# An opening on a fixed plan: eight units of attention ahead of the steps, engines in program order up to chunk 2

## The chip, the core and the metric

The kernel runs on one core of a Trainium2 chip. The metric is device time in microseconds (us). The median of three runs of the kernel before is 949.6 us (948.06 to 950.32). One further execution was recorded by the profiler; all durations and waits below are from it.

## What is computed

Windowed attention over 8 sequences of 576 tokens with 8 heads of 64 channels, followed by a feed-forward layer on the 4608 tokens:

```python
rel = pos[:, None] - pos[None, :]
mask = (rel >= 0) & (rel < 64)
scores = np.where(mask, scale * np.matmul(q, k.transpose(0, 1, 3, 2)), -1e9)
scores = scores - np.max(scores, axis=-1, keepdims=True)
attn = np.exp(scores)
attn = attn / (np.sum(attn, axis=-1, keepdims=True) + 1e-09)
x = np.matmul(attn, v)                      # to (4608 tokens, 512 channels)
h = x @ w_in                                # (512, 2048), drawn as float64
g = h * np.tanh(softplus(h))                # Mish
out = (g @ w_out).astype(np.float32)        # (2048, 512), float64
```

## The kernel before

**Chunks, units, steps.** The tokens are cut into 12 chunks of 384. A chunk's attention is four *units*, one for each pair of heads (NPAIR = 4). Its feed-forward part is 16 *steps*, one for each 128 rows of the hidden layer (NF = 16).

**A unit** is: TensorE makes six 128x128 squares of scores in PSUM (tile `s_ps`); VectorE adds the mask, scales, and keeps the row minimum (L148); ScalarE takes the exponential and the row sums (L151); VectorE adds 1e-9 to the sums, inverts them and multiplies (L155 to L157); the probabilities `pr` are transposed into `pT`; TensorE multiplies by V into `o_ps`; ScalarE rounds the result to `xh` (L250), and VectorE forms the rest `xl` (L251). The transposition is six TensorE transposes into `t_ps` with one copy by ScalarE and one by VectorE (L239, L240) in chunks 0 to 2. From chunk 3 on it is one VectorE transpose of 32x32 blocks into `tr` and twelve DMAs that move the blocks to `pT` (L190, L232).

**A step** has a first half (`ffn_in`): 12 matmuls of 384 columns into `h_ps`, namely xh and xl against the high part of w_in, and xh against its low part. ScalarE then computes Mish twice (`t`, L266, and its rounded `gh`, L267), and GpSimd the difference `gl` (L268). The second half (`ffn_out`, called by `flush`) is 9 matmuls of 512 columns into the accumulators `acc`. It runs LAG = 2 steps behind the first half.

**Weights.** They arrive as float64 in 32 *pieces* of 128x512, 16 of w_in and 16 of w_out, in staging tiles `st`. A piece is turned into two float32 tiles by five bit operations (`wa`, L298 to L303; the one at L299 is on GpSimd for a w_in piece, on VectorE for a w_out piece), one rounding on ScalarE (`wi_h` or `wo_h`, L304) and one subtraction (`wi_l` on VectorE, `wo_l` on GpSimd, L305).

**PSUM** has eight banks: three for the accumulators `acc0` to `acc2`, two for `h_ps`, three called `at`. Chunk 1's accumulators lie in the three `at` banks, since the steps of chunks 0 and 1 alternate and share the weights as they come.

**What sets the order.** The opening calls chunk 0's four units one after another; then HEAD = 5 steps of chunk 0 run alone while chunk 1's units are planned between them, and then steps of chunks 0 and 1 alternate: (0, f), (1, f - 5). Two pieces of weights are started at each step of chunk 0. Chunk 2's units are planned over the last steps of chunk 1. Up to there the tile framework's scheduler decides where an instruction stands in its engine's queue, with priorities (`high_priority`) as hints; only TensorE's steps are tied to the order of the program, through `in_order` once `ordered` is set. Every load goes through SyncE's queue. Chunks 3 to 11 follow the event list (`plan`, `plan_runs`).

Of the kernel before, what the change touches and what calls it, by code (L numbers as in the profile page):

```python
# [27 lines left out]
def tile_window_attn_mish_ffn(  # L28
# [109 lines left out]
    def probs(c, s_ps, turns):  # L138

        pr = ap_.tile([P, HM, P], F32, name="pr", bufs=2)  # L140
        mx = ap_.tile([P, HM], F32, name="mx", bufs=3)
        sm = ap_.tile([P, HM], F32, name="sm", bufs=3)
        for turn in turns:
            js = [h * NM + m for h, m in turn]
            for j, (h, m) in zip(js, turn):
                first = [(c * NB + 2 * m + par) % blocks_per_seq == 0 for par in range(2)]
                mk = firsts[first.index(True)] if any(first) else mask
                nc.vector.tensor_tensor_reduce(  # L148
                    out=pr[:, j, :], in0=s_ps[h][m], in1=mk,
                    op0=ALU.add, op1=ALU.min, scale=-0.125, scalar=3.0e38, accum_out=mx[:, j:j + 1])  # L150
                nc.scalar.activation(pr[:, j, :], pr[:, j, :], AF.Exp, bias=mx[:, j:j + 1], scale=-1.0,  # L151
                                     accum_out=sm[:, j:j + 1])
            js = slice(min(js), max(js) + 1)
            w = js.stop - js.start
            nc.vector.tensor_scalar(sm[:, js], sm[:, js], 1e-9, None, ALU.add)  # L155
# [352 lines left out]
```

## Time and profile before

| what | value |
|---|---|
| median of three runs | 949.6 us |
| the profiled execution | 949.47 us |
| its span, first to last instruction | 947.2 us |
| TensorE busy | 913.1 us, 96% of the span |
| VectorE busy | 312.3 us, 33% |
| ScalarE busy | 404.6 us, 43% |
| GpSimd busy | 241.9 us, 26% |
| start of the first `h_ps` matmul | 38.14 us |
| start of chunk 2's first `h_ps` matmul | 209.78 us |
| start of chunk 3's first `s_ps` matmul | 222.46 us |

PE is TensorE, PEld its loads of the stationary operand, DVE VectorE, ACT ScalarE, POOL GpSimd and SP SyncE. In the rows, a time in front is a start in us from the span's start, and the next number a length in us. A group's row gives busy us and mean ns of one, then idle time just before them and what ended it. Starts of neighbouring matmuls lie closer than their lengths, since matmuls are pipelined; the time that a run of them takes is read from start to start. Each float32 matmul of the attention stands twice in the trace (24 for the 12 of a unit).

### The profile page before, as it was taken

To read this page: it belongs to the slowest core of one execution; us is meant where nothing else is said; L and a number is where in the kernel's file an instruction comes from. 1 tells how busy PE (TensorE), PEld (TensorE's weight loads), DVE (VectorE), ACT (ScalarE), POOL (GpSimd) and SP (SyncE) were. 2 spreads that over 40 slices of the span, in tenths; PEclk is the share of its full clock that TensorE was granted. 3 is DMA by queue.
4 is the path that set the end of the run, shared out by engine and by line. 5 is a ranking of instruction groups with operands and counts; after the bars stand their busy time and mean duration, and the time that the engine had idled before them with its cause. 6 is when DMAs were issued, how large, how long until landed. Compare 5 with 4: busy or idle time off the path is not lost.

```text
span 947.2 us, 16773 instructions
## 1 busy us (share of the span) xinstructions
PE 913.1 (96%) x6408; PEld 816.2 (86%) x6408; DVE 312.3 (33%) x1016; ACT 404.6 (43%) x1116; POOL 241.9 (26%) x241
## 2 busy tenths in 40 slices
PE   4679999999999999999999999999999999999998
PEld 3568999878889999999999999999999999999997
DVE  6899885242331321312303303303203213210000
ACT  4574333565662543534525525525425435332211
POOL 2233565202112222222222222222122222222221
PEclk9779999999999999999999999999999999999999
DMA  7554441141331221212213204203302312200000
GB/s 252 157 198 144 134 133 45 54 120 63 94 105 59 84 80 62 80 55 90 78 29 117 75 23 123 75 26 94 106 26 84 114 27 81 82 26 1 34 1 34
DMA packets 82639, 77.26 MB, mean 82 GB/s; under 512 B 10368, under 2 KB 73856, under 8 KB 82560
## 3 DMA queue, kind: packets, MB, share of 16 engines
q1 hardware_dynamic: 77376, 66.75, 23.1%
q10 hardware_dynamic: 5184, 9.44, 2.7%
q8 instruction: 51, 0.84, 0.4%
q14 instruction: 28, 0.23, 0.1%
HBM read 56.10 MB, written 9.44 MB: 69 GB/s over the span
## 4 chain that ended last, share of the span: by engine, by line
PE 92%; DVE 5%; ACT 1%; SPq 1%; DMA 1%; issue 0%; ACTq 0%; DVEq 0%
PE h_ps L96 42%; PE acc L96 42%; PE o_ps L96 4%; PE s_ps L96 4%; DVE pr L157 1%; DVE pr L148 1%; DVE wa L302 1%; DVE wa L303 1%; ACT pr L151 1%; SPq L190 0%; PE t_ps L239 0%; DVE wi_l L305 0%; DMA k_t<-kT 0%; DVE wa L301 0%; ACT L266 0%
## 5 line engine op out<-in xcount | busy, mean ns | idle before, releaser
L268 POOL TENSOR_TENSOR gl<-t,gh 128x384 fp32r<-128x384 f32 x192 | 199.7, 1040 | 615.0 <-ACT gh L267 605.1
L266 ACT ACTIVATE t<-h_ps 128x384 f32<-128x384 f32 x192 | 94.4, 492 | 421.0 <-PE h_ps L96 405.9
L96 PE MATMUL h_ps<-xh,wi_h 128*128 128x384 f32 x768 | 261.2, 340 | 0.0
L96 PE MATMUL h_ps<-xh,wi_l 128*128 128x384 f32 x768 | 260.0, 339 | 0.0
L96 PE MATMUL h_ps<-xl,wi_h 128*128 128x384 f32 x768 | 259.0, 337 | 0.0
L96 PE MATMUL acc<-wo_h,gh 128*128 128x512 f32 x576 | 229.1, 398 | 0.0
L96 PE MATMUL acc<-wo_l,gh 128*128 128x512 f32 x576 | 227.5, 395 | 0.0
L96 PE MATMUL acc<-wo_h,gl 128*128 128x512 f32 x576 | 224.6, 390 | 0.0
L96 PEld LDWEIGHTS h_ps<-xh,wi_h 128*128 128x128 f32 x768 | 145.0, 189 | 9.3 <-issue 0.7
L96 PEld LDWEIGHTS h_ps<-xl,wi_h 128*128 128x128 f32 x768 | 145.1, 189 | 7.0
L96 PEld LDWEIGHTS h_ps<-xh,wi_l 128*128 128x128 f32 x768 | 144.9, 189 | 0.0
L96 PEld LDWEIGHTS acc<-wo_h,gl 128*128 128x128 f32 x576 | 108.6, 188 | 24.4 <-issue 0.2
L96 PEld LDWEIGHTS acc<-wo_h,gh 128*128 128x128 f32 x576 | 108.3, 188 | 20.8 <-issue 3.6
L96 PEld LDWEIGHTS acc<-wo_l,gh 128*128 128x128 f32 x576 | 108.6, 189 | 14.9
L151 ACT ACTIVATE pr<-pr,mx 128x128 f32<-128x128 f32 x288 | 111.7, 389 | 14.4 <-DVE mx L148 14.1
L219 DVE CAST xh<-o_ps 128x256 fp32r<-128x256 f32 x16 | 6.8, 425 | 326.9 <-PE o_ps L96 326.9
L267 ACT ACTIVATE gh<-h_ps 128x384 fp32r<-128x384 f32 x192 | 93.2, 485 | 0.0
L148 DVE CUSTOM_DVE_ANT_0 pr<-s_ps,mask 128x128 f32<-128x128 f32 x288 | 63.6, 285 | 32.0 <-PE s_ps L96 32.0
L286 DVE COPY o<-acc 128x512 f32<-128x512 f32 x12 | 8.3, 691 | 185.5 <-PE acc L96 185.5
L96 PE MATMUL s_ps<-k_t,q_t 64*64 64x128 f32 x1152 | 47.0, 291 | 11.8 <-DMA k_t<-kT 9.7
L151 ACT ACTIVATION_READ_ACCUMULATOR pr<-pr,mx 128x1 f32 x288 | 53.9, 187 | 0.0
L96 PEld LDWEIGHTS o_ps<-pT,v_t 128*64 128x64 f32 x1152 | 39.9, 146 | 15.6 <-issue 8.1
(43 smaller groups left out, 547.9 us busy)
## 6 DMA issues: line engine op xcount, KB each, us to landing
v_t<-vN SPq DMA_DIRECT2D x48, 384.0 KB, 4.0
k_t<-kT SPq DMA_DIRECT2D x47, 224.0 KB, 4.4
pT<-tr SPq DMA_DIRECT2D x432, 24.0 KB, 1.8
out<-o ACTq DMA_DIRECT2D x36, 256.0 KB, 2.3
q_t<-qT SPq DMA_DIRECT2D x47, 192.0 KB, 4.3
st<-w_in SPq DMA_DIRECT2D x16, 512.0 KB, 4.3
st<-w_out SPq DMA_DIRECT2D x16, 512.0 KB, 3.3
q_t<-qT SPq DMA_DIRECT2D x3, 64.0 KB, 2.1
```

The lines of the kernel that those rows point to most:

```text
L96: order.append(nc.tensor.matmul(*args, **kw).ins)
L148: nc.vector.tensor_tensor_reduce(out=pr[:, j, :], in0=s_ps[h][m], in1=mk, op0=ALU.add, op1=ALU.min, scale=-0.125, scalar=3.0e38, accum_out ...
L151: nc.scalar.activation(pr[:, j, :], pr[:, j, :], AF.Exp, bias=mx[:, j:j + 1], scale=-1.0, accum_out=sm[:, j:j + 1])
L157: nc.vector.tensor_tensor(pr[:, js, :], pr[:, js, :], sm[:, js].unsqueeze(2).to_broadcast([P, w, P]), ALU.mult)
L219: nc.vector.tensor_copy(xh[:, :cut], o_ps[0])
L266: nc.scalar.activation(t, h_ps, AF.Mish)
L267: nc.scalar.activation(gh, h_ps, AF.Mish)
L268: nc.gpsimd.tensor_tensor(gl, t, gh.bitcast(F32), ALU.subtract)
L286: nc.vector.tensor_copy(o, acc[t])
L302: nc.vector.scalar_tensor_tensor(a, hi, 0xC0000000, a, ALU.bitwise_and, ALU.bitwise_or)
L303: nc.vector.scalar_tensor_tensor(a, lo, 29, a, ALU.logical_shift_right, ALU.bitwise_or)
```

## The change

The first part of the program is written out in the order in which it is to run, and each instruction on VectorE, ScalarE, GpSimd and SyncE that goes through the wrapper `InTurn` keeps its place on its engine (`keep_in_program_order`) as long as `held[0]` is set, that is through step 31. TensorE is tied to the program's order from its first matmul.

The eight units of chunks 0 and 1 come first, in one loop over u. In turn u, VectorE masks unit u, finishes `xl` of unit u - 2, converts weight piece u and normalizes unit u; ScalarE rounds `xh` of unit u - 2, takes four exponentials of unit u, makes both copies of unit u - 1's transposes, and then the other two exponentials; TensorE makes the scores of unit u + 1, the values of unit u - 1 and the transposes of unit u. The first halves of steps 0 and 1 stand in turns 6 and 7. Steps of chunks 0 and 1 alternate from step 2 on (HEAD = 2). Each step converts one piece, and all VectorE work on it: the bit operations and the subtraction that GpSimd did have moved there, save one bit operation (`Abs`), which ScalarE does in the opening. Eight pieces are converted in the opening and 24 in steps 0 to 23.

Chunk 2's scores stand after steps 8, 11, 17 and 20, in the two `h_ps` banks, with an extra `flush` behind them; its exponentials come in two batches of twelve, at steps 11 and 20. Its transposes are VectorE's, at steps 14, 17, 22 and 24, so that 24 TensorE transposes fall away and 48 small DMAs are added. Its values come at steps 29 to 32.

```diff
     order = []
     ordered = []
+    held = [True]
+
...
+        def __getattr__(self, name):
+            call = getattr(self.engine, name)
+
+            def issue(*args, **kw):
+                i = call(*args, **kw)
+                if held[0]:
+                    tc.keep_in_program_order(i)
+                return i
+            return issue
+
+    vec, act, pool, load = (InTurn(e) for e in (nc.vector, nc.scalar, nc.gpsimd, nc.sync))
...
     def in_order():
-        return tc.issue_after(order[-1]) if ordered else nullcontext()
-
-
-
-
-    sums = itertools.cycle([f"acc{t}" for t in range(NTT)])
-
-    def bank(c, p, name):
-        if c == 2 or (c == 0 and p % 2 == 0):
-            return ps_acc.tile([P, CH], F32, name=name, tag=next(sums))
+        return tc.issue_after(order[-1]) if order else nullcontext()
+
+
+
+
+    def acc_bank(t, name):
+        return ps_acc.tile([P, CH], F32, name=name, tag=f"acc{t}")
+
+    def h_bank(name):
+        return ps_h.tile([P, CH], F32, name=name, tag="h_ps")
+
+    def at_bank(name):
         return ps_at.tile([P, CH], F32, name=name, tag="at")
...
+    def masked(c, unit, s_ps, squares_, exps=True):
+        pr, mx, sm = unit
+        for h, m in squares_:
+            j = h * NM + m
+            first = [(c * NB + 2 * m + par) % blocks_per_seq == 0 for par in range(2)]
+            mk = firsts[first.index(True)] if any(first) else mask
+            vec.tensor_tensor_reduce(
+                out=pr[:, j, :], in0=s_ps[h][m], in1=mk,
+                op0=ALU.add, op1=ALU.min, scale=-0.125, scalar=3.0e38, accum_out=mx[:, j:j + 1])
+            if exps:
+                exp(unit, [(h, m)])
...
-    def run_transpose(pr):
-        pT = next(pTs)
-        tr = mp.tile([P, P // 32, HM, 32], F32, name="tr", tag="st", bufs=3)
-        nc.vector.transpose(tr.rearrange("p k j i -> p j k i"), pr.rearrange("p j (k i) -> p j k i", i=32))
+    def run_transpose(pr, pT=None):
+        tr = mp.tile([P, P // 32, HM, 32], F32, name="tr", tag="st", bufs=3) if pT is None else             ap_.tile([P, P // 32, HM, 32], F32, name="tr", tag="v_t", bufs=2)
+        pT = pT or next(pTs)
+        vec.transpose(tr.rearrange("p k j i -> p j k i"), pr.rearrange("p j (k i) -> p j k i", i=32))
         return pT, moves(pT, tr)
+
+    def spare_pT():
+        pT = mp.tile([P, P // 32, HM, 32], F32, name="pT", tag="st", bufs=3)
+        pool.memset(pT, 0.0)
+        return pT
...
+    def te_transpose(pr, banks):
+        pT = next(pTs)
+        banks = [squares(b) for b in banks]
+        for h, t_ps in enumerate(banks):
             for m in range(NM):
                 order.append(nc.tensor.transpose(t_ps[:, m, :], pr[:, h * NM + m, :], ident).ins)
-            (nc.scalar.copy if h == 0 else nc.vector.tensor_copy)(
-                pT[:, :, h * NM:(h + 1) * NM, :].rearrange("p r m i -> p m r i"),
-                t_ps.rearrange("p m (r i) -> p m r i", i=32))
+        return pT, banks
+
+    def te_copies(pT, banks, by):
+        for h, (t_ps, copy) in enumerate(zip(banks, by)):
+            copy(pT[:, :, h * NM:(h + 1) * NM, :].rearrange("p r m i -> p m r i"),
+                 t_ps.rearrange("p m (r i) -> p m r i", i=32))
...
-        nc.vector.tensor_scalar(a, hi, 0x7FFFFFFF, None, ALU.bitwise_and)
-        (nc.gpsimd if first else nc.vector).tensor_scalar(af, af, BIG, TINY, ALU.min, ALU.max)
-
-        nc.vector.tensor_scalar(a, a, 3, 0x3FFFFFFF, ALU.logical_shift_left, ALU.bitwise_and)
-        nc.vector.scalar_tensor_tensor(a, hi, 0xC0000000, a, ALU.bitwise_and, ALU.bitwise_or)
-        nc.vector.scalar_tensor_tensor(a, lo, 29, a, ALU.logical_shift_right, ALU.bitwise_or)
-        nc.scalar.copy(wh, af)
-        (nc.vector if first else nc.gpsimd).tensor_tensor(wl, af, wh.bitcast(F32), ALU.subtract)
...
+        if by_act:
+            act.activation(af, hi.bitcast(F32), AF.Abs)
+        else:
+            vec.tensor_scalar(a, hi, 0x7FFFFFFF, None, ALU.bitwise_and)
+        worked.append((lo, hi, a, af, wh, wl))
+
+    def w_bits(parts=range(4)):
+
+        if not worked:
+            return
+        lo, hi, a, af, wh, wl = worked[0]
+        for part in parts:
+            if part == 0:
+                vec.tensor_scalar(af, af, BIG, TINY, ALU.min, ALU.max)
+            elif part == 1:
+                vec.tensor_scalar(a, a, 3, 0x3FFFFFFF, ALU.logical_shift_left, ALU.bitwise_and)
+            elif part == 2:
+                vec.scalar_tensor_tensor(a, hi, 0xC0000000, a, ALU.bitwise_and, ALU.bitwise_or)
+            else:
+                vec.scalar_tensor_tensor(a, lo, 29, a, ALU.logical_shift_right, ALU.bitwise_or)
+                rounded.append([af, wh, wl, False])
+                worked.pop(0)
+
+    def w_round():
+        for r in rounded:
+            if not r[3]:
+                act.copy(r[1], r[0])
+                r[3] = True
+
+    def w_rest():
+        while rounded and rounded[0][3]:
+            af, wh, wl, _ = rounded.pop(0)
+            vec.tensor_tensor(wl, af, wh.bitcast(F32), ALU.subtract)
...
-    HEAD = 5
+    HEAD = 2
...
+    def products_of(u):
+        a, p = units[u]
+        if u == 0:
+            banks = [b for t in range(NM) for b in ([acc_bank(0, "s_ps"), acc_bank(1, "s_ps")], [at_bank("s_ps"), at_bank("s_ps")],
+                                                     [h_bank("s_ps"), h_bank("s_ps")])[t]]
+        elif u % 2 == 0:
+            banks = [acc_bank(t, "s_ps") for t in range(2)]
+        else:
+            banks = [at_bank("s_ps") for _ in range(2)]
+        a.products(p, banks)
+        if u + 2 < U + 2:
+            a.load(p + 2, "qk")
+
+    def values_of(u):
+        a, p = units[u]
+        o_ps = (at_bank if u == U - 1 else lambda n: acc_bank(2, n))("o_ps")
+        outs[u] = o_ps
+        with in_order():
+            value_products(a.v[p], a.pT.pop(p), [o_ps[:, n:n + BLK] for n in range(0, CH, BLK)])
+        if u + 2 < U:
+            a.load(p + 2, "v")
...
-    take_w(1)
+    w_load()
     atts[0].load(1, "qk")
     atts[0].load(0, "v")
-    take_w(1)
+    w_load()
     atts[0].load(1, "v")
-    ev = []
-    for p in range(NPAIR):
-        ev += [(p, 2, atts[0].scores, p), (p + 0.75, 1, atts[0].transpose, p), (p + 1.25, 0, atts[0].values, p)]
-    for at, _, fn, p in sorted(ev, key=lambda e: e[:2]):
-        fn(p)
-        if at == p and p > 0:
-            take_w(1)
-    atts[1].plan(0, 2 * HEAD / (NPAIR + 1), 1, 1.5)
-    atts[2].plan(third, (starts[2] - third) / (NPAIR + 1), 1, 1.5)
-
+    w_load()
+
...
+    products_of(0)
+    for u in range(U + 1):
+        now = u < U
+        if u > 1:
+            rest_high(u - 2)
+        if now:
+            a, p = units[u]
+            squares_ = BY_PAIR if u == 0 else BY_HEAD
+            a.masked(p, squares_, exps=False)
+            exp(a.pr[p], squares_[:4])
+        if u == 0:
+            w_abs(False)
+        if u > 1:
+            rest_low(u - 2)
+        if u + 1 < U:
+            products_of(u + 1)
+        if u > 0:
+            units[u - 1][0].te_copies(units[u - 1][1], (act.copy, act.copy))
+            values_of(u - 1)
+        if u >= EARLY and len(early) < HEAD:
+            early.append(first_half(len(early)))
+        if now:
+            exp(a.pr[p], squares_[4:])
+        if u == U - 1:
+            for n, h_ps in enumerate(early):
+                step(n, h_ps)
+        w_bits([0])
+        w_rest()
+        w_bits([1, 2])
+        n = normal_parts(u) if now else iter(())
+        next(n, None)
+        w_bits([3])
+        next(n, None)
+        if u == U:
+            rest_high(u - 1)
+            rest_low(u - 1)
+        if u + 1 not in WITHOUT:
+            w_abs(u + 1 < U)
+            w_load()
+        next(n, None)
+        w_round()
+        if now:
+            a.te_transpose(p, [at_bank("t_ps") if u == U - 1 else acc_bank(h, "t_ps") if u == U - 2 else h_bank("t_ps") for h in range(2)])
 
...
+    third = atts[2]
+    SCORES = [8, 11, 17, 20]
+    MOVED = [14, 17, 22, 24]
+
+    def between(n):
+
+        if n in SCORES:
+            p = SCORES.index(n)
+            third.products(p, [h_bank("s_ps") for _ in range(2)])
+            third.load(p + 2, "qk")
+            with in_order():
+                flush()
+            third.masked(p, BY_HEAD, exps=False)
+            if p % 2:
+                third.exp(p - 1)
+                third.exp(p)
+                third.normal(p - 1)
+                third.normal(p)
+        if n in MOVED:
+            p = MOVED.index(n)
+            third.dve_transpose(p, p > 1)
+
     for n, (c, f) in enumerate(steps):
...
+        if n == starts[2] // 2:
+            held[0] = True
+            third.values(NPAIR - 1, h_bank)
+            with in_order():
+                flush()
+            held[0] = False
+        if n >= HEAD:
+            step(n)
         run(2 * n)
+        if held[0]:
+            w_round()
+            w_bits()
+            w_abs(False)
+            w_load()
+            if last - 3 <= n < last - 1:
+                third.load(n - last + 3, "v")
+            if last < n < last + NPAIR:
+                third.values(n - last - 1, h_bank)
         if len(pend) > LAG:
             with in_order():
                 flush()
+        if held[0]:
+            between(n)
+            w_rest()
         run(2 * n + 1)
-        if c == 0:
-            take_w(2)
```

What this makes of the queues is shown at three places. In these rows a tile's number tells buffers apart, and all instructions that pass through the wrapper carry its line, L106. `ISA pr,mx` is the masking of one square.

TensorE, the opening. Before:

```order
L96 MATMUL s_ps<-k_t,q_t 64x128 x24
L239 MATMUL t_ps<-ident,pr 128x128 x6
L96 MATMUL s_ps<-k_t,q_t 64x128 x12
L96 MATMUL o_ps<-pT_106,v_t 64x64 x12
L239 MATMUL t_ps<-ident,pr 128x128 x6
L96 MATMUL o_ps<-pT_107,v_t 64x64
L96 MATMUL s_ps<-k_t,q_t 64x128 x12
L96 MATMUL o_ps<-pT_107,v_t 64x64 x11
L239 MATMUL t_ps<-ident,pr 128x128 x6
```

TensorE, the same place, changed:

```order
L115 MATMUL s_ps<-k_t,q_t 64x128 x24
L288 MATMUL t_ps<-ident,pr 128x128 x6
L115 MATMUL s_ps<-k_t,q_t 64x128 x12
L115 MATMUL o_ps<-pT_106,v_t 64x64 x12
L288 MATMUL t_ps<-ident,pr 128x128 x6
L115 MATMUL s_ps<-k_t,q_t 64x128 x12
L115 MATMUL o_ps<-pT_107,v_t 64x64 x12
L288 MATMUL t_ps<-ident,pr 128x128 x6
```

The scores of unit u + 1 now always stand between the transposes and the values of unit u - 1, and the round repeats for eight units instead of four.

VectorE, a stretch of the opening that ends with the normalization of a unit. Before, in chunk 0's third unit:

```order
L298 TENSOR_SCALAR wa<-st 128x512
L305 TENSOR_TENSOR wi_l<-wa,wi_h 128x512
L301 TENSOR_SCALAR wa<-wa 128x512
L157 TENSOR_TENSOR pr<-pr,sm 128x384
L155 TENSOR_SCALAR sm<-sm 128x3
L251 TENSOR_TENSOR xl_245<-o_ps,xh_244 128x384
L302 SCALAR_TENSOR_TENSOR wa<-st,wa 128x512
L298 TENSOR_SCALAR wa<-st 128x512
```

VectorE, the third unit in the changed kernel, from behind its six masked squares:

```order
L106 TENSOR_TENSOR xl_293<-o_ps,xh_292 128x384
L106 TENSOR_SCALAR wa<-wa 128x512
L106 TENSOR_TENSOR wi_l<-wa,wi_h 128x512
L106 TENSOR_SCALAR wa<-wa 128x512
L106 SCALAR_TENSOR_TENSOR wa<-st,wa 128x512
L106 TENSOR_SCALAR sm<-sm 128x6
L106 SCALAR_TENSOR_TENSOR wa<-st,wa 128x512
L106 RECIPROCAL sm<-sm 128x6
L106 TENSOR_TENSOR pr<-pr,sm 128x768
```

The normalization is one pass over six squares instead of two over three, and the operations on one piece stand between `xl` and the normalization, one piece to a unit.

VectorE, steps 7 and 8 of the changed kernel (nothing in the kernel before answers to this place, since chunk 2's scores stood behind the last piece):

```order
L106 TENSOR_TENSOR wo_l<-wa,wo_h 128x512
L106 TENSOR_SCALAR wa<-wa 128x512 x2
L106 SCALAR_TENSOR_TENSOR wa<-st,wa 128x512 x2
L106 TENSOR_SCALAR wa<-st 128x512
L106 ISA pr,mx<-s_ps,mask 128x128
```

Six masked squares then stand between the bit operations of one piece and the subtraction of the piece before it. On TensorE, everything from chunk 3's first scores on stands in the same order in both kernels, row for row.

More of the change, by code (lines that the diff above doesn't have):

```diff
@@ L136, in products @@
                q_t[rows, n * BLK:(n + 1) * BLK], k_t[rows, n * BLK:n * BLK + P], start=True, stop=True)
[L138 to L155, printed above, removed]
-            nc.vector.reciprocal(sm[:, js], sm[:, js])
-            nc.vector.tensor_tensor(pr[:, js, :], pr[:, js, :], sm[:, js].unsqueeze(2).to_broadcast([P, w, P]), ALU.mult)
-        return pr
@@ L162, in squares, with probs, score_products @@
+    def probs(c, s_ps, squares_):
+        unit = new_probs()
+        masked(c, unit, s_ps, squares_)
+        normal(unit, squares_)
+        return unit[0]
+    BY_HEAD = [(h, m) for h in range(2) for m in range(NM)]
+    BY_PAIR = [(h, m) for m in range(NM) for h in range(2)]
     def squares(bank_):
         return bank_.rearrange("p (m k) -> p m k", k=P)
-    def att_scores(c, p, tiles):
-        s_ps = [squares(bank(c, p, "s_ps")) for _ in range(2)]
-        s_ps = [[s[:, m, :] for m in range(NM)] for s in s_ps]
+    def score_products(tiles, banks):
+        if len(banks) == 2:
+            s_ps = [squares(b) for b in banks]
+            s_ps = [[s[:, m, :] for m in range(NM)] for s in s_ps]
+        else:
+            s_ps = [[squares(banks[2 * m + h])[:, 0, :] for m in range(NM)] for h in range(2)]
@@ L168, in att_scores @@
         for m in range(NM):
             products(tiles, m, [s[m] for s in s_ps])
-        return probs(c, s_ps, HEADS if c == 0 else [sum(HEADS, [])])
+        return s_ps
+    def att_scores(c, p, tiles):
+        return probs(c, score_products(tiles, [at_bank("s_ps") for _ in range(2)]), BY_HEAD)
     def run_scores(c, qk):
@@ L419, in tile_window_attn_mish_ffn @@
         steps += [(0, f), (1, f - HEAD)]
-    third = 2 * len(steps) + 2
+    last = len(steps) - 2
     steps += [(1, f) for f in range(NF - HEAD, NF)]
@@ L428, in tile_window_attn_mish_ffn, with first_half, step @@
+    def first_half(n):
+        c, f = steps[n]
+        with in_order():
+            return ffn_in(c, atts[c].x, f)
+    def step(n, h_ps=None):
+        pend.append((*steps[n], function(h_ps or first_half(n))))
     atts[0].load(0, "qk")
[L429 removed]
+    w_load()
     atts[0].load(1, "qk")
     atts[0].load(0, "v")
[L432 removed]
+    w_load()
     atts[0].load(1, "v")
[L434 to L436 removed]
```

168 lines of the change are left out of this document (112 added, 56 removed).

## The prediction

> **What bounds the kernel now.** I read the page first, then the busy times by stretch, then TensorE's waits up to chunk 3.
>
> ```profile
> PE   4679999999999999999999999999999999999998
> PEclk9779999999999999999999999999999999999999
> ```
>
> The 40 slices show one engine at its limit from about 75 us on, TensorE. Only the first three slices leave it idle, and there its granted clock is low as well. Stretches cut at the changes of the clock:
>
> ```profile
> 0.00:27.20 27.20, 13.94 (x159) 10.09 (x159) 19.67 (x76) 11.31 (x43) 7.64 (x21) 1.00 0.73 232
> 30.60:40.80 10.20, 7.94 (x62) 6.75 (x63) 7.42 (x18) 4.89 (x11) 2.32 (x2) 0.50 0.56 179
> 71.50:74.90 3.40, 3.40 (x9) 2.33 (x8) 3.40 (x19) 2.60 (x13) 0.33 (x1) 0.51 0.41 130
> 74.90:180.00 105.10, 105.10 (x573) 95.16 (x572) 73.83 (x105) 35.29 (x75) 53.20 (x44) 1.00 0.32 105
> sum 222.40, PE 193.97 PEld 167.74 DVE 151.79 ACT 109.98 POOL 82.29; mean PE 21.55 PEld 18.64 DVE 16.87 ACT 12.22 POOL 9.14
> ```
>
> Columns: length, then busy us (and instructions) of PE, PEld, DVE, ACT and POOL, then clock, DMA share, GB/s. Up to 222.4 us, where chunk 3's first scores start, TensorE idles 222.4 - 194.0 = 28.4 us. Part of its busy time runs at half clock (the first record of the clock is at 27.2 us; before that the matmuls' own times show it):
>
> ```profile
> 9.21 1.56 PE L96 MATMUL s_ps<-k_t,q_t 64*64 64x128 f32 x24 [2.01 <-DMA k_t<-kT]
> 10.71 1.54 PE L239 MATMUL t_ps<-ident,pr 128*128 128x128 f32 x6
> 16.17 1.55 PE L96 MATMUL o_ps<-pT,v_t 128*64 128x64 f32 x24
> 41.65 0.89 PE L96 MATMUL s_ps<-k_t,q_t 64*64 64x128 f32 x24
> 14.69 1.56 PE L96 MATMUL s_ps<-k_t,q_t 64*64 64x128 f32 x24 [2.44 <-DMA k_t<-kT]
> 202.40 2.11 PE h_ps L96 x12
> 204.51 0.85 PE o_ps L96 x24
> 207.47 0.82 PE L239 MATMUL t_ps<-ident,pr 128*128 128x128 f32 x6
> 212.14 2.06 PE acc L96 x9
> 222.46 0.78 PE L96 MATMUL s_ps<-k_t,q_t 64*64 64x128 f32 x20
> ```
>
> A unit's scores take 1.56 us early on and 0.89 us at full clock, its values 1.55 against 0.85, its transposes 1.54 against 0.82. A step is 2.11 + 2.06 = 4.17 us. The work up to 222.4 us at full clock is 35 first halves, 33 second halves, and 12 units of 0.89 + 0.85 + 0.82: 73.9 + 68.0 + 30.7 = 172.6 us. So 50 us are lost there, 28 idle and 22 to the clock and to small gaps. The waits to that point (us in all, times, longest):
>
> ```profile
> PE s_ps L96 <- DMA k_t<-kT: 9.7, 4, 3.7
> PE t_ps L239 <- DVE pr L157: 8.0, 5, 4.1
> PE t_ps L239 <- DVE sm L155: 3.5, 1, 3.5
> PE o_ps L96 <- ACT pT L240: 3.1, 2, 2.8
> ```
>
> After the first loads, TensorE waits for VectorE's normalization (L155 to L157). What lies behind 222.46 us stands in the same order on TensorE in both kernels, so the change is worth what it moves that one start.
>
> **The opening.** Durations of single operations, not stretched by another engine:
>
> ```profile
> 8.63 0.42 DVE L298 TENSOR_SCALAR wa<-st 128x512 uint32<-128x512 uint32 x1
> 13.11 0.69 DVE L303 SCALAR_TENSOR_TENSOR wa<-st,wa 128x512 uint32<-128x512 uint32 x1
> 15.31 0.65 DVE L305 TENSOR_TENSOR wi_l<-wa,wi_h 128x512 fp32r<-128x512 f32 x1
> L157 DVE TENSOR_TENSOR pr<-pr,sm 128x768 f32<-128x768 f32 x4 | 3.8, 951 | 0.0
> L155 DVE TENSOR_SCALAR sm<-sm 128x6 f32<-128x6 f32 x12 | 2.1, 171 | 21.2 <-ACT pr L151 21.2
> L156 DVE RECIPROCAL sm<-sm 128x6 f32<-128x6 f32 x12 | 2.3, 188 | 0.4
> L251 DVE TENSOR_TENSOR xl<-o_ps,xh 128x384 fp32r<-128x384 f32 x8 | 4.5, 557 | 14.4 <-ACT xh L250 14.4
> 7.36 0.29 DVE L148 CUSTOM_DVE_ANT_0 pr<-s_ps,mask 128x128 f32<-128x128 f32 x1 [7.36 <-PE s_ps L96]
> 8.42 0.08 DVE L148 DVE_READ_ACCUMULATOR2_ANT mx<- 128x1 f32 x1
> ```
>
> Six masked squares take 8.63 - 7.36 = 1.27 us. VectorE's list for one unit is then 1.27 (masks) + 0.56 (xl) + 2 x 0.42 + 2 x 0.69 + 0.65 (piece) + 0.17 + 0.19 + 0.95 (normalization) = 6.0 us. ScalarE's rows:
>
> ```profile
> 8.10 0.39 ACT L151 ACTIVATE pr<-pr,mx 128x128 f32<-128x128 f32 x1
> L240 ACT COPY pT<-t_ps 128x384 f32<-128x384 f32 x8 | 3.8, 474 | 1.1 <-PE t_ps L239 1.1
> L250 ACT CAST xh<-o_ps 128x384 fp32r<-128x384 f32 x8 | 3.8, 473 | 6.8 <-PE o_ps L96 6.8
> L304 ACT CAST wi_h<-wa 128x512 fp32r<-128x512 f32 x10 | 6.2, 622 | 9.6 <-DVE wa L303 9.6
> L266 ACT ACTIVATE t<-h_ps 128x384 f32<-128x384 f32 x11 | 5.4, 489 | 2.9 <-PE h_ps L96 1.7 <-DVE wi_l L305 1.1
> L266 ACT ACT_TABLE_LOAD x5 | 6.4, 1283 | 2.3 <-PE h_ps L96 2.3
> ```
>
> Per unit ScalarE has 6 x 0.39 + 2 x 0.47 + 0.47 + 0.62 + `Abs`. No row shows `Abs` on ScalarE; between its pass over 512 columns at L304 and twice that, 0.6 to 1.2 us, I take 0.6, the nearest, and either end leaves ScalarE at 5.0 to 5.6, below 6.0. TensorE at half clock needs 1.56 + 1.55 + 1.5 = 4.6. Between two normalizations lies one round trip: transposes 1.5, behind them copies that stand behind four exponentials (2.0 to 2.9), two more exponentials and the read-out of their sums (3.9), while VectorE comes to the sums at 0.3 + 1.27 + 0.56 + 0.42 + 0.65 + 0.42 + 0.69 = 4.3 or somewhat sooner. The trip just fits: VectorE sets the pace, 6.0 us a unit.
>
> The first units are slower. Unit 0: the last loads end its masks near 7.7, and the first piece is used at 8.63 now; I take 8.2 and add 4.0 (one 0.42 more than the list from the piece on), 12.2. Unit 1 has no xl: 17.7. Unit 2's q and k, for which TensorE waited until 14.69, now queue behind one more piece of 0.52 MB, 2.3 us at the 232 GB/s of that stretch (0 if they start before it, in which case this unit gains 2 us); its scores end at 14.7 + 2.3 + 1.5 = 18.5. Unit 0's values stand behind them and end at 20.0; `xh`, four exponentials, two copies and two exponentials follow on ScalarE to 24.0, the rest of the normalization and of the piece to 26.1. Units 3 to 6 at 6.0 bring 50.1.
>
> The end of the opening: step 0's first half stands before unit 6's transposes and holds them 1.4 us; then transposes 0.8, copies 1.0, two exponentials 1.0, the table load 1.28, two pairs of Mish 2.0, xh 0.5, copies 1.0, values 0.85: 9.7 us, so step 2 could start at 59.8. The row at 71.50 shows the clock at half over 3.4 us of full work after a stretch with short idle gaps; the opening has gaps of 1 to 2 us, so I add one such stretch, half of 3.4, 1.7: **61.5 us**.
>
> The Trainium skill, "TensorE: Matmul & The Clock Gate", section "HAM oscillation — how this bites in real kernels", lets the clock fall only after an idle window of about 3.4 us. By it the 1.7 would be 0 and the time 941.7 us. The row at 71.50, behind a stretch in which TensorE was busy 11.4 of 13.6 us, speaks against it; no run here shows the changed opening.
>
> **From there to chunk 3.** 33 first halves and 33 second halves, four scores and four values of chunk 2 and about 0.4 us of switches: 69.6 + 68.0 + 7.0 + 0.4 = 145.0 us of TensorE, if nothing makes it wait.
>
> VectorE can. Per step it has 3 x 0.42 + 2 x 0.69 + 0.65 = 3.3 us on a piece, against 4.17. But GpSimd's `gl` falls between:
>
> ```profile
> 106.14 1.19 POOL L268 TENSOR_TENSOR gl<-t,gh 128x384 fp32r<-128x384 f32 x1
> 106.49 1.12 DVE L301 TENSOR_SCALAR wa<-wa 128x512 uint32<-128x512 uint32 x1
> L232 DVE STREAM_TRANSPOSE tr<-pr 128x768 f32<-128x768 f32 x4 | 3.9, 978 | 0.1
> ```
>
> The bit operation, 0.42 alone, took 1.12 beside it: 0.7 us for one `gl`. With one `gl` a step VectorE needs 4.0 us. The bound below is 3.3 (gl always falls beside something else), above 4.3 (all of a gl's 1.0 us is added).
>
> All is in one queue, so VectorE masks chunk 2's scores only after the bit operations of that step, and the scores hold both `h_ps` banks: TensorE's next first half waits. Let T be the start of step 2. VectorE ends the bits of step 0 at T + 4.2 (xh, xl, then 0.42 and 2.2), those of step 8 at T + 4.2 + 8 x 4.0 = T + 36.2, and three masked squares 1.1 later, T + 37.3. TensorE wants the bank at T + 6 x 4.17 + 2.11 + 2 x 2.06 + 0.9 = T + 32.2. **Wait 5.1.** At step 11: 3 x 4.0 + 1.27 = 13.3 against 3 x 4.17 + 0.9 = 13.4, no wait. There VectorE also waits for twelve exponentials (ScalarE ends them 2.6 behind the bank), normalizes twice 1.3 and subtracts; step 12's bits end 7.6 behind. Step 17: 7.6 + 5 x 4.0 + 0.98 (transpose) + 1.1 = 29.7 against 6 x 4.17 + 0.8 = 25.8. **Wait 3.9.** Step 20: 12.0 + 1.27 + 0.98 = 14.25 against 13.3. **Wait 0.95.** Sum 10.0. ScalarE's four table loads (1.28) lie in the two steps before a bank is needed again. Each VectorE transpose puts twelve DMAs on SyncE's queue ahead of the next piece's load; the piece is used two steps later, 8 us, and the moves have five steps or more, so both are covered. GpSimd's two clearings of `pT` come when the pieces are done. Chunk 2's values stand behind second halves that cover their copies.
>
> **Sum.** 61.5 + 145.0 + 10.0 = 216.5 against 222.46: 6.0 us. The profiled execution took 949.47 (span 947.2 and 2.3 around it, 0.1 below the median of the runs), so **943.4 us**.
>
> **Rivals.**
> 1. *VectorE is never late.* With 3.3 us a step, the bits of step 8 and the masks end at T + 31.7, before T + 32.2, and the other two in time too. The 10.0 go: 933.4. For it: VectorE idles beside the steps now (73.8 of 105.1 busy). Against it: the stretched 1.12.
> 2. *Each `gl` blocks VectorE wholly.* With 4.3 us the waits are 7.5 + 0.8 + 5.7 + 1.9 = 15.9, and nothing is left of the gain: 949.3. The Trainium skill, "SBUF — State Buffer", section "Who interferes with whom", says that VectorE and GpSimd lock a shared port pair for a whole instruction and that the other fully blocks. By that rule it is this case; the trace has 0.7 for one pair.
> 3. *Slower: the round trip, not VectorE's list, sets the pace of a unit.* It fits by under half a us.
>
> ```profile
> 38.14 0.69 PE L96 MATMUL h_ps<-xh,wi_h 128*128 128x384 f32 x1
> ```
>
> Before, four units took 38.14 - 7.36 = 30.8, 7.7 each, with VectorE waited for. At 7.7 us units 1 and 3 to 6 cost 1.6 + 4 x 1.7 = 8.4 more, and a clock that stays at half through the last units up to 2.8: 951.8 to 954.6, about 953. It decides from 7.2 us a unit on, where 5 x 1.2 us have spent the gain of 6.0.
>
> **Numbers.** Forecast 0.50 (937 to 947.6), rival 1 0.18, rival 2 0.14, rival 3 0.18. About 0.2% (1.9 us) is what a measurement can tell from no change: faster 0.50 + 0.18 = 0.68, same 0.14, slower 0.18. From 933 to 952 leaves out the tails of rivals 1 and 3, 0.05 and 0.12.
>
> **What would show it.** Masks of one unit to masks of the next 6.0 us apart, and no wait of VectorE at the sums; step 2's first half at 61.5; waits of TensorE for VectorE's masks before steps 9, 18 and 21, of 5, 4 and 1 us; chunk 3's first scores at 216.5. A unit of over 7 us or a late load in units 3 to 6 breaks the first term; waits at every step would mean ScalarE's rounding, which stands before the next Mish and behind the bits, holds the step.

## The result, and the profile after

The changed kernel takes 941.38 us (median of five runs, 939.15 to 944.2), the kernel before 949.6 (five runs, 948.06 to 950.39): a ratio of 0.9918, 95% interval 0.9895 to 0.9941. It is faster by 0.8%, 2.0 us below the forecast of 943.4. The profiled execution took 941.38 us with a span of 939.6, so it stands at the median.

The busy line and the clock line of the page after:

```profile
PE   4698989999999999999999999999999999999998
PEclk9899989999999999999999999999999999999999
```

A slice is 23.5 us. The opening now leaves TensorE idle in two slices instead of three. New are an 8 in the busy line at 70 to 94 us and again at 117 to 141, there with a lower clock. TensorE's waits up to chunk 3 (us in all, times, longest):

```profile
PE s_ps L115 <- DMA k_t<-kT: 9.7, 3, 3.7
PE t_ps L288 <- DVE pr L106: 8.2, 5, 2.0
PE h_ps L115 <- DVE mx L106: 6.9, 2, 3.8
PE o_ps L115 <- ACT pT L106: 3.4, 5, 1.1
PE o_ps L115 <- ACT gh L106: 1.0, 1, 1.0
```

The third row is the new wait that the prediction spoke of: a first half waits for the row minima `mx`, the output of the masks. Three rows of TensorE and the stretches around those waits (length, busy us of PE, PEld, DVE, ACT, POOL, then clock, DMA share, GB/s):

```profile
55.34 0.45 PE L115 MATMUL h_ps<-xh,wi_h 128*128 128x384 f32 x1
91.25 0.41 PE L115 MATMUL h_ps<-xh,wi_h 128*128 128x384 f32 x1 [3.10 <-DVE mx L106]
136.87 0.66 PE L115 MATMUL h_ps<-xh,wi_h 128*128 128x384 f32 x1 [3.79 <-DVE mx L106]
```

```profile
0.00:55.34 55.34, 33.77 (x456) 26.90 (x456) 43.35 (x167) 39.89 (x138) 6.14 (x19) 0.94 0.72 230
55.34:215.08 159.74, 151.86 (x887) 135.46 (x885) 111.90 (x218) 62.66 (x153) 38.41 (x35) 0.97 0.36 116
88.35:91.76 3.41, 0.51 (x3) 0.54 (x4) 3.34 (x17) 0.00 (x0) 0.00 (x0) 1.00 0.51 171
91.76:95.18 3.42, 3.42 (x13) 3.42 (x12) 3.07 (x6) 0.10 (x1) 0.00 (x0) 0.50 0.64 242
132.72:136.14 3.42, 0.36 (x2) 0.00 (x0) 2.09 (x5) 0.00 (x0) 0.00 (x0) 1.00 0.84 322
136.14:139.55 3.41, 2.68 (x8) 2.71 (x9) 3.38 (x16) 0.00 (x0) 0.00 (x0) 0.50 0.70 263
```

Step 2 starts at 55.34 us (forecast 61.5). Steps 9 and 18 wait for masks, as forecast, and behind both waits TensorE runs at half clock, which was not forecast: once for 3.4 us, once for 6.8. Chunk 3's first scores start at 215.08 us instead of 222.46, 7.4 us earlier; the span is 7.6 shorter. What lies behind is the same. Up to chunk 3 TensorE idles no less than before: 215.08 - 33.77 - 151.86 = 29.5 us against 28.4. Its busy time fell, from 194.0 us to 185.6. Of these 8.4 us the 24 transposes that fell away are 3.3. The clock stands at half for 17.1 us up to there, against 23.9 before, in records that begin at 20.1 and at 27.2 us; how much of the rest that explains was not worked out.

VectorE's rows for one turn of the opening (start, length; the other five masked squares and the rest of the turn left out):

```profile
35.25 0.28 DVE L106 CUSTOM_DVE_ANT_0 pr<-s_ps,mask 128x128 f32<-128x128 f32 x1
...
36.52 0.55 DVE L106 TENSOR_TENSOR xl<-o_ps,xh 128x384 fp32r<-128x384 f32 x1
36.99 0.42 DVE L106 TENSOR_SCALAR wa<-wa 128x512 f32<-128x512 f32 x1
37.32 0.68 DVE L106 TENSOR_TENSOR wo_l<-wa,wo_h 128x512 fp32r<-128x512 f32 x1
37.92 0.42 DVE L106 TENSOR_SCALAR wa<-wa 128x512 uint32<-128x512 uint32 x1
38.38 0.69 DVE L106 SCALAR_TENSOR_TENSOR wa<-st,wa 128x512 uint32<-128x512 uint32 x1
...
40.80 0.28 DVE L106 CUSTOM_DVE_ANT_0 pr<-s_ps,mask 128x128 f32<-128x128 f32 x1
```

From masks to masks it is 5.55 us, and no row has a wait. The prediction added lengths and got 6.0. But in this list an operation that doesn't need the one before it starts before that one has ended: `xl` is 0.55 long, and the next row starts 0.47 behind its start. One that does need it doesn't: the row at 38.38 takes the result of the row at 37.92, which ends at 38.34.

### The profile page after: what moved, and what is told of

It is laid out like the page before. It is cut to its first block, busy times and chain, and to the rows that moved or that the text cites. A ratio compares the mean times of both kernels' runs of the same rounds, so it can differ in the third digit from the quotient of the medians.

```text
span 939.6 us, 16749 instructions
## 1 busy us (share of the span) xinstructions
PE 904.7 (96%) x6384; PEld 810.8 (86%) x6384; DVE 315.8 (34%) x1022; ACT 397.1 (42%) x1116; POOL 204.1 (22%) x211
## 4 chain that ended last, share of the span: by engine, by line
PE 85%; DVE 8%; DMA 2%; ACT 2%; SPq 2%; issue 1%; ACTq 0%
PE h_ps L115 40%; PE acc L115 38%; DVE wa L106 6%; PE o_ps L115 4%; PE s_ps L115 3%; SPq L106 2%; DMA st<-w_out 1%; ACT pr L106 1%; DVE pr L106 1%; DMA k_t<-kT 1%; DVE wo_l L106 0%; DVE wi_l L106 0%; ACT L106 0%; DVE xl L106 0%; DVE tr L106 0%
## 5 line engine op out<-in xcount | busy, mean ns | idle before, releaser
L106 POOL TENSOR_TENSOR gl<-t,gh 128x384 fp32r<-128x384 f32 x192 | 198.3, 1033 | 726.0 <-ACT gh L106 710.5
L106 ACT ACTIVATE t<-h_ps 128x384 f32<-128x384 f32 x192 | 94.4, 492 | 447.8 <-PE h_ps L115 433.1
L106 ACT ACTIVATE pr<-pr,mx 128x128 f32<-128x128 f32 x288 | 111.7, 390 | 6.3 <-DVE mx L106 6.0
L106 ACT ACTIVATE gh<-h_ps 128x384 fp32r<-128x384 f32 x192 | 93.2, 485 | 0.0
L106 DVE CUSTOM_DVE_ANT_0 pr<-s_ps,mask 128x128 f32<-128x128 f32 x288 | 63.2, 286 | 24.6 <-PE s_ps L115 19.5
L106 DVE SCALAR_TENSOR_TENSOR wa<-st,wa 128x512 uint32<-128x512 uint32 x64 | 54.1, 845 | 2.0
L106 ACT ACTIVATION_READ_ACCUMULATOR pr<-pr,mx 128x1 f32 x288 | 54.1, 188 | 0.0
```

What stands on the lines that cost most here:

```text
L106: i = call(*args, **kw)
```

## Experiments

Each changes the new kernel. "The change" below is that kernel, at 941.38 us. The diffs are shortened, and their comments are added here.

**1. The masks ahead of the bits** (`masks_first`).

```diff
             w_round()
+            scored(n)      # in steps 8, 11, 17, 20: flush, scores, flush, masks
             w_bits()
...
     def between(n):
         if n in SCORES:
             p = SCORES.index(n)
-            third.products(p, [h_bank("s_ps") for _ in range(2)])
-            third.load(p + 2, "qk")
-            with in_order():
-                flush()
-            third.masked(p, BY_HEAD, exps=False)
```

> Edit: in steps 8, 11, 17 and 20 the scores, the extra second half and VectorE's masks stand ahead of that step's bit operations instead of behind them; nothing else moves. Theory (the masks queue behind bits that nobody needs yet): the masks of steps 8 and 17 start near 87.3 and 132.3 us instead of 90.39 and 136.01, TensorE's waits for them (6.9 us in 2) fall under 1 us in all, and the half clock behind them (4.4 us) goes with them: chunk 3's first scores near 204 to 205 instead of 215.1, time 930 to 931 instead of 941.4. Rival A (VectorE is late as a whole, the order is indifferent): the bits come late instead, TensorE then waits for a weight or for Mish behind a rounding, and less than 3 us are gained: over 938. Rival B (the half clock has nothing to do with the waits): it stays, 934.5 to 935.

Measured: 933.82 us (933.58 to 934.43), ratio to the kernel before 0.9839 (0.9824 to 0.9854). The masks start at 87.39 and 129.44 us. TensorE's waits from step 2 to chunk 3:

```profile
PE h_ps L115 <- DVE mx L106: 2.4, 3, 1.0
PE o_ps L115 <- ACT gh L106: 1.4, 1, 1.4
PE h_ps L115 <- ACT gh L106: 0.8, 1, 0.8
```

Of 6.9 us for masks 2.4 are left, none over 1.0, and the clock stays at full through the steps. Chunk 3's scores start at 208.33. The theory holds in kind; it promised 3 us too much, since some lateness stays.

**2. Without GpSimd's subtraction** (`no_gl`).

```diff
+            if held[0]:
+                return gh, gh
             pool.tensor_tensor(gl, t, gh.bitcast(F32), ALU.subtract)
```

> Edit: in the steps of chunks 0 and 1 GpSimd's subtraction for gl is left out, and the matmul that takes gl takes gh (that part of the output is another one; all lengths and other orders stay). Theory (one gl stretches VectorE by 0.69 us, and that makes the masks late): VectorE's step falls from 3.88 to 3.2 us, the masks of steps 8 and 17 are no longer waited for, nor does the clock fall behind them: about 930. Rival (the bit operations are long for another reason, as their operands or the DMAs into SBUF): VectorE's step stays at 3.8 to 3.9 us and the time at 940 to 942.

Measured: 930.87 us in one run. First the change, on VectorE and GpSimd, then this kernel:

```profile
72.97 1.06 POOL L106 TENSOR_TENSOR gl<-t,gh 128x384 fp32r<-128x384 f32 x1 [2.83 <-ACT gh L106]
73.19 2.12 DVE L106 SCALAR_TENSOR_TENSOR wa<-st,wa 128x512 uint32<-128x512 uint32 x2
```

```profile
71.77 1.42 DVE L106 SCALAR_TENSOR_TENSOR wa<-st,wa 128x512 uint32<-128x512 uint32 x2
73.44 0.69 DVE L106 TENSOR_TENSOR wi_l<-wa,wi_h 128x512 fp32r<-128x512 f32 x1
76.63 0.69 DVE L106 TENSOR_TENSOR wo_l<-wa,wo_h 128x512 fp32r<-128x512 f32 x1
```

The pair of bit operations falls from 2.12 to 1.42, and the step (one subtraction to the next) from 3.88 to 76.63 - 73.44 = 3.19. That is 0.69 us for one `gl`, as taken. One wait for a mask is left, of 1.2 us. From step 2 to chunk 3's scores it takes 148.7 us instead of 159.7, which shows what VectorE's lateness costs with the clock behind it: some 11 us.

**3. One more operation in the opening** (`opening_extra`).

```diff
             if part == 0:
-                vec.tensor_scalar(af, af, BIG, TINY, ALU.min, ALU.max)
+                for _ in range(2 if opening[0] else 1):
+                    vec.tensor_scalar(af, af, BIG, TINY, ALU.min, ALU.max)
```

> Edit: in the opening each piece's first bit operation (min and max, 0.42 us) is done twice. Theory (VectorE's list sets the pace of a unit): units 3 to 7 go from 5.55 to 5.95 us, step 2 starts 2.1 to 2.9 us later, at 57.5 to 58.3, time 943.5 to 944.5. Rival (the round trip over TensorE and ScalarE sets it, and VectorE has room): the pace stays at 5.55 and the time at 941.4.

Measured: 945.06 us in one run. Masks of units 3 and 4 (in this kernel the wrapper is line L107):

```profile
25.89 0.28 DVE L107 CUSTOM_DVE_ANT_0 pr<-s_ps,mask 128x128 f32<-128x128 f32 x1
...
31.91 0.28 DVE L107 CUSTOM_DVE_ANT_0 pr<-s_ps,mask 128x128 f32<-128x128 f32 x1
```

The pace is 6.02, and step 2 comes at 59.03, 3.7 us later. The list sets the pace: from the masks of unit 3 to step 2 it takes 33.1 us instead of 31.2, 1.9 more for four operations. The other 1.7 us lie in the first three units and need not come from the extra operation. These units vary from execution to execution: in the nine traces with the same opening (the change and the runs of experiments 1, 2 and 4 to 8) unit 3's masks start between 23.8 and 26.0 us.

**4. The moves in fours** (`moves_split`).

```diff
             between(n)
+            move_some(4 if n < 22 else 12)   # moves of chunk 2's transposes, from a list
             w_rest()
```

> Edit: the twelve moves of chunk 2's first two transposes are issued four to a step, each four behind that step's load of a piece, and no longer twelve in a row (8.02 us on SyncE's queue from 123.77 on) ahead of the load. Theory (those moves held the load of the piece that VectorE waited 1.26 us for): that wait goes, and TensorE's wait before step 18 falls from 3.8 to 2.5 us. If the clock falls only behind waits of over about 3 us, the half clock behind this one (2.8 us) goes too: 937 to 937.6. If any wait of over 2 us does it: 940 to 940.3. Rival (the load was late for the width of the DMA engines, not the queue): no change, 941.4.

Rows of the change, SyncE's queue and VectorE, show what this was about:

```profile
123.77 8.02 SPq L106 DMA_DIRECT2D pT<-tr  x12
131.88 0.53 SPq L106 DMA_DIRECT2D st<-w_out  x1
```

```profile
135.67 0.43 DVE L106 TENSOR_SCALAR wa<-st 128x512 uint32<-128x512 uint32 x1 [1.26 <-DMA st<-w_out]
```

Measured: 938.72 us (937.84 to 939.33), ratio 0.9887 (0.987 to 0.9903). VectorE's wait for w_out is gone; the wait before step 18 is 2.6 instead of 3.8. Its interval overlaps that of the change a little, so the 2.7 us are likely, not certain. Half clock still follows, for one stretch instead of two:

```profile
133.85:137.26 3.41, 1.12 (x6) 1.15 (x7) 3.38 (x16) 0.00 (x0) 0.00 (x0) 1.00 0.58 187
137.26:140.67 3.41, 3.41 (x12) 3.41 (x12) 3.31 (x7) 1.18 (x3) 0.18 (x1) 0.50 0.56 200
```

So the length of the wait alone does not decide on the clock; more on this below.

**5. Chunk 2's transposes back on TensorE** (`te_third`).

```diff
-            third.dve_transpose(p, p > 1)
+            third.te_transpose(p, [h_bank("t_ps") for _ in range(2)], spare_pT() if p > 1 else None)
+            third.te_copies(p, (act.copy, act.copy))
```

> Edit: chunk 2's four transposes go back to TensorE, at the same four steps, into the two h_ps banks, with both copies on ScalarE; VectorE's four transposes and the 48 moves fall away. Theory (what TensorE saved, VectorE and SyncE's queue gave back): TensorE gets 4 x 0.82 us more and waits some 0.6 us four times for the copies, 5.7 us; the load is no longer behind twelve moves and VectorE has 0.98 us less ahead of the masks, so TensorE's wait before step 18 falls from 3.8 to about 1.6 and the half clock behind it (2.8 us) goes, 5.0 us: 941 to 943, about no change. Rival (the moved transposes are worth their 3.3 us of TensorE and cost nothing elsewhere): 945 to 947.

Measured: 943.38 us in one run, within the spread of the change. From step 2 to chunk 3's scores it takes 216.47 - 56.14 = 160.3 us against 159.7. New is a wait for the copies, of 4.5 us:

```profile
PE h_ps L115 <- ACT pT L106: 4.5, 4, 1.9
```

Against it stands a shorter wait before step 18 (0.2 us), and less half clock, one stretch (at 158.88) for three. So in one run moving the transposes was no gain: what it took off TensorE, VectorE's and SyncE's lateness gave back. The wait before step 9 is as long as in the change, 3.13 us, and yet no half clock follows:

```profile
92.04 0.41 PE L115 MATMUL h_ps<-xh,wi_h 128*128 128x384 f32 x1 [3.13 <-DVE mx L106]
```

```profile
87.20:90.61 3.41, 1.72 (x8) 1.07 (x6) 3.31 (x7) 0.63 (x1) 0.00 (x0) 1.00 0.43 154
90.61:94.03 3.42, 1.99 (x11) 2.02 (x12) 3.35 (x18) 0.00 (x0) 0.00 (x0) 1.00 0.60 193
```

Here the wait falls on two stretches of the clock's records, and TensorE is busy for half of each.

**6. The fixed order only in the opening** (`untied`).

```diff
-                if held[0]:
+                if tied[0]:        # cleared ahead of step 2
                     tc.keep_in_program_order(i)
```

> Edit: the opening keeps its fixed order; from step 2 on the scheduler places the instructions of VectorE, ScalarE, GpSimd and SyncE, as it does in the kernel before. TensorE's order stays. The masks of chunk 2 then stand behind most bits of the next pieces. Theory (only where the masks stand counts, not that the order is fixed): TensorE's waits for the masks are as long or longer, step 2 near 55.3 us as before, time 941 to 946, so that nearly the whole gain over the kernel before is the opening's. Rival (the fixed order through the steps is itself worth several us): over 947.

Measured: 939.09 us in one run, at the lower edge of the change's spread and outside both expectations. Step 2 starts at 55.31, and from there to chunk 3's scores it is 157.5 us. The masks come no earlier (91.15 us against 90.39). But ScalarE's Mish comes later too, so that half of the scores waits for `gh`: at step 8, 1.03 us there and 2.27 at the next first half, in place of one wait of 3.10. So the lateness is cut into waits of at most 2.3 us, and no half clock follows in the steps. As far as one run shows, the fixed order from step 2 on is not what the change gains by.

**7. The subtraction on VectorE** (`gl_vec`).

```diff
-            pool.tensor_tensor(gl, t, gh.bitcast(F32), ALU.subtract)
+            lows.append((gl, t, gh))       # steps 2 to 26
...
             w_load()
+            low()                          # vec.tensor_tensor(gl, t, gh, subtract)
```

> Edit: in steps 2 to 26 VectorE does the subtraction for gl, behind that step's bits, in place of GpSimd. Theory (a gl on GpSimd costs VectorE more than a gl on VectorE): 0.69 us of stretch go and about 0.5 us come (0.65 x 384/512), VectorE's step falls from 3.88 to 3.65 to 3.75 us, the masks of step 8 come 1 to 1.5 us earlier, the waits before steps 9 and 18 fall under 2.5 us and the half clock behind them goes: 933 to 936. Rival (VectorE then waits for ScalarE's Mish in its queue): the step stays at 3.9 or grows, 941 or more.

Measured: 935.39 us in one run. VectorE's step is 78.26 - 74.60 = 3.66 us:

```profile
74.13 0.55 DVE L106 TENSOR_TENSOR gl<-t,gh 128x384 fp32r<-128x384 f32 x1
74.60 0.68 DVE L106 TENSOR_TENSOR wi_l<-wa,wi_h 128x512 fp32r<-128x512 f32 x1
...
78.26 0.69 DVE L106 TENSOR_TENSOR wo_l<-wa,wo_h 128x512 fp32r<-128x512 f32 x1
```

The same subtraction costs VectorE 3.66 - 3.19 = 0.47 us a step when VectorE does it and 0.69 when GpSimd does. A wait before step 18 is left (2.9 us by the trace) without half clock, again since it falls on two stretches; that part of the gain is luck.

**8. Three of them together** (`mf_split_gl`: 1, 4 and 7), timed twice.

> Edits of masks_first, moves_split and gl_vec together. Theory: what masks_first left (waits for masks 2.4 us, for Mish behind a late rounding 0.8 and for the values 1.4) shrinks by about 2 to 3 us as VectorE is no longer late: 930.5 to 932. Rival (the rest is not VectorE's lateness): 933.5 to 934.

> The kernel of mf_split_gl once more, for a comparison with skip_two on the same chip: 931 to 934.

Measured: 932.42 us (ratio 0.9814, 0.9801 to 0.9828) and 932.39 (0.9824, 0.9811 to 0.9838). TensorE no longer waits for a mask; from step 2 to chunk 3's scores it takes 149.9 us.

**9. Two turns without weights** (`skip`).

```diff
-        w_bits([0])
+        piece = u not in (4, 5)
+        if piece:              # so too w_bits([1, 2]), w_bits([3]), w_abs and w_load
+            w_bits([0])
```

> Edit: no piece of weights is converted in turns 4 and 5 of the opening; the 24 pieces behind them come two steps later each. VectorE's list in those turns is then 1.27 + 0.56 + 1.31 = 3.1 us (in turn 4 also one subtraction, 3.8), far below the round trip, so that these two units show what the round trip over TensorE and ScalarE takes by itself. Theory (VectorE's list sets 5.55 us, the round trip is a little shorter): masks of these units to those of the next 4.0 to 4.9 us apart, VectorE waits at the sums there, step 2 starts 1.3 to 3.1 us earlier, at 52.2 to 54.0. Rival 3 of the prediction (the round trip sets the pace): 5.5 us or more apart, step 2 at 55 as before.

Measured: 942.27 us in one run. VectorE's masks of units 4, 5 and 6, and one of its waits at the sums:

```profile
29.83 0.28 DVE L106 CUSTOM_DVE_ANT_0 pr<-s_ps,mask 128x128 f32<-128x128 f32 x1
...
34.73 0.28 DVE L106 CUSTOM_DVE_ANT_0 pr<-s_ps,mask 128x128 f32<-128x128 f32 x1
...
38.31 0.17 DVE L106 TENSOR_SCALAR sm<-sm 128x6 f32<-128x6 f32 x1 [1.77 <-ACT pr L106]
...
39.62 0.28 DVE L106 CUSTOM_DVE_ANT_0 pr<-s_ps,mask 128x128 f32<-128x128 f32 x1
```

The round trip alone takes 4.9 us a unit, below the list's 5.55. Step 2 starts at 53.96; from unit 3's masks to it the run takes 29.7 us instead of 31.2, 1.5 less, as the theory had it. The total shows nothing of it: TensorE waits 2.8 us at the first values of chunk 2, and half clock follows.

**10. All four** (`skip_all`), **and moves on two queues** (`skip_two`).

> Edits of mf_split_gl and skip together. Theory: step 2 comes 1.3 to 3.1 us earlier and VectorE, with 3.66 us a step against TensorE's 4.17, still has the pieces in time: 929.5 to 931.1 against 932.4. Rival (a piece that comes two steps later makes a first half wait for its weight): no gain, 932 to 935.

Measured: 935.39 us (0.9855, 0.9836 to 0.9874), no gain, but not for the rival's reason: no first half waits for a weight. TensorE waits at the first values, and SyncE's queue tells why. The columns are start, length and count:

```profile
160.51 15.74 SPq L106 DMA_DIRECT2D pT<-tr  x24
176.30 10.43 SPq L106 DMA_DIRECT2D v_t<-vN  x4
```

```profile
180.17 0.92 PE L115 MATMUL o_ps<-pT,v_t 128*64 128x64 f32 x24 [3.15 <-issue]
```

The trace can name no releaser ("issue"); the load of V started at 176.30 behind 24 moves. The moves were late because GpSimd may clear the buffers for `pT` only when the last pieces, now two steps later, are done with them: the clearings, at 159.53 and 163.18, both waited for VectorE's `wa`.

```diff
-            moved.append(load.dma_start(...))
+            queue = pool if pT is not pTs_[0] and pT is not pTs_[1] and len(left) % 2 else load
+            moved.append(queue.dma_start(...))
```

> Edits of skip_all, and of the 24 moves of chunk 2's last two transposes every second one is started from GpSimd's queue. Theory (in skip_all 24 moves took 15.74 us on SyncE's queue and held the loads of chunk 2's V until 176.30; TensorE then waited 3.15 us at the first values): with half of them elsewhere the loads start near 168, that wait goes, and what skip gained in the opening is left: 929 to 931. Rival (the two-queue moves are no faster, as the DMA engines or GpSimd's own issue cost are the limit): the wait stays, 933 to 935.5.

Measured: 931.15 us (930.22 to 932.86), ratio 0.9812 (0.9799 to 0.9826). The loads start 6 us earlier and the wait is gone:

```profile
160.88 9.05 SPq L107 DMA_DIRECT2D pT<-tr  x12
170.24 18.88 SPq L107 DMA_DIRECT2D v_t<-vN  x5
```

It is the fastest kernel here, 1.9% below the kernel before. That it beats `mf_split_gl` (1.2 us on the same chip) is not certain, since the intervals overlap. The traces agree with it: from step 2 to chunk 3 both take 149.9 to 150.0 us, and from unit 3's masks to step 2 it is again 29.7.

## Why the prediction came out near

Sign and size were right, within 2.0 us of time and 1.4 us of the start of chunk 3 (forecast 216.5, measured 215.08). But this is two errors that nearly cancel, which is luck: the opening was 6.2 us better than forecast, the steps behind it 4.7 worse (159.74 against 155.0).

1. **The opening's bound: right.** VectorE's list sets the pace (experiments 3 and 9), and rival 3, the round trip, is 0.65 us a unit below it. **Its size was off.** The term of 6.0 us a unit added lengths where starts count: 5.55, or 1.8 us over units 3 to 6. Units 0 to 2 ended 2.0 us earlier (24.15 against 26.1). The first piece was used at 7.04 instead of 8.2, but nothing of that was left at the end of unit 1 (18.02, forecast 17.7). Unit 2 gained it: its load came 1.0 us later than before, not 2.3, and its scores ended at 17.2 instead of 18.5. The nine traces have 23.8 to 26.0 for this end, so some of the 2.0 is chance. The tail took 9.0 instead of 9.7 (the terms given for it add up to 9.8). And the 1.7 us for a half-clock stretch did not come: no stretch of the tail had more than 1.1 us idle. Half clock stood twice before it, from 30.3 and from 40.6 us, where VectorE's list sets the pace and it cost nothing that the rows show. Sum 1.8 + 2.0 + 0.7 + 1.7 = 6.2.
2. **TensorE's work, 145.0 us: too small by 2.4.** Its busy time from 55.34 to 215.08 is 151.86, of which 4.4 us belong to the half clock; 147.4 are left. The term that was mis-sized is the 0.4 us for all switches between kinds of matmul: chunk 2's first scores take 1.09 us to the next matmul instead of 0.89, and the second half behind them 2.18 instead of 2.06. In all it is some 0.4 us at each of the four scores and 0.2 at each of the four values.
3. **The masks queue behind the bits: right, shown by experiment 1.** Waits before steps 9, 12, 18 and 21 were forecast as 5.1, 0, 3.9 and 0.95; measured 3.1, 0, 3.8 and 0. The first was 2.0 too long: the bits of step 8 ended 35.05 us behind step 2's start instead of 36.2 (a step is 3.88, not 4.0, and one step met no `gl`), three masks took 0.8 instead of 1.1, and TensorE came for the bank at 32.8 instead of 32.2.
4. **0.7 us for one `gl`: right, 0.69** (experiment 2). Rival 2 had VectorE lose the whole `gl`, 1.06 us here. Its price is wrong, but its mechanism is in the rows of the change:

```profile
96.09 1.01 POOL L106 TENSOR_TENSOR gl<-t,gh 128x384 fp32r<-128x384 f32 x1 [10.42 <-ACT gh L106]
96.50 1.15 DVE L106 TENSOR_TENSOR wo_l<-wa,wo_h 128x512 fp32r<-128x512 f32 x1 [1.56 <-ACT wo_h L106]
102.38 2.10 DVE L106 SCALAR_TENSOR_TENSOR wa<-st,wa 128x512 uint32<-128x512 uint32 x2
102.49 1.44 POOL L106 TENSOR_TENSOR gl<-t,gh 128x384 fp32r<-128x384 f32 x1 [3.15 <-ACT gh L106]
```

The `wo_l` starts under a `gl`, takes 1.15 us instead of 0.69 and ends 0.55 behind the `gl`, so it stood nearly until the `gl` was through. The other way round, the `gl` at 102.49 starts under an operation of VectorE and takes 1.44 instead of 1.01. In the steps a `gl` costs less than its length because its first 0.22 us (72.97 to 73.19 in experiment 2) fall beside an operation that VectorE has already begun, and the last 0.14 (0.69 - 0.55) are not waited for: 1.06 - 0.22 - 0.14 = 0.70. The Trainium skill, "SBUF — State Buffer", section "Who interferes with whom", says that the two engines share a port pair as an exclusive lock, and that whoever issues first has it for the whole instruction; the rows above agree. Neither the prediction's 0.7 for one pair nor the 0.69 speaks against that rule. Rival 1, VectorE never late, is what experiment 8 made: 932.4, forecast 933.4, again with an earlier step 2 and longer steps than forecast.
5. **SyncE's moves "are covered": wrong.** The prediction weighed the time until the moves were needed, and the next piece's two steps of 8 us, but not how long the queue itself is held: twelve moves take 8.02 us there. It made 1.2 us of the wait before step 18 (3.8, and 2.6 in experiment 4), so that the near hit of 3.9 is partly chance.
6. **The clock behind the waits: missed.** 4.4 us (steps 9, 10, 18 and 19 took 1.4, 0.2, 1.9 and 0.95 us more than 2.11 each for their first halves). The prediction put one half-clock stretch into the opening, and none behind the waits of 5.1 and 3.9 us that it had itself forecast.
7. The wait at chunk 2's values, called covered, was 1.0 us.

Against 10.0 us of waits, the runs show 7.9 idle (159.74 - 151.86), 4.4 of clock and 2.4 of switches, 14.7 in all: 4.7 more. What the gain over the kernel before comes from is only in part shown. The steps' fixed order (`untied`) and the moved transposes (`te_third`) can each be undone at no loss that one run shows, which leaves the opening as the likely source. The opening by itself was not tried: without the new alternation of steps (HEAD = 2), without chunk 2's earlier scores, or without the work that moved from GpSimd to VectorE.

## What to carry to other kernels

When an order is fixed by hand, place what another engine waits for (here masks that hold PSUM banks) ahead of work that nobody needs yet, and count what each queue holds, the DMA queue's issue times too. Add an engine's list from start to start, not by lengths. A wait of a few us on TensorE costs more than itself if it leaves the engine idle for half of one of the 3.41 us stretches on which its clock changes.
